# A frequency filter with a SwiGLU layer behind it: other filter tiles, a third stage-A buffer, moved x loads, and a last step in halves

## The chip, the cores and the metric

The kernel runs on one core of a Trainium2 chip, in a single launch. The metric is the device time of that core in microseconds (us). Engines are named as in the profile: PE is TensorE, with PEld for its weight loads, DVE is VectorE, ACT is ScalarE, POOL is GpSimd and SP is SyncE, which here only issues transfers. PSUM is the memory that PE writes its results to; SBUF is the memory that the engines share.

## What is computed

The input x has 8 sequences of 3008 rows by 256 columns. Each sequence is filtered in the frequency domain, then every row goes through an RMS norm and a SwiGLU layer of width 1536:

```python
X = np.fft.rfft(x, axis=1)                 # 8 x 1505 x 256
Y = X * (filt_r + 1j * filt_i)[None]       # filters: 1505 x 256
y = np.fft.irfft(Y, n=3008, axis=1).reshape(8 * 3008, 256)
xn = y / np.sqrt(np.mean(y * y, axis=-1, keepdims=True) + 1e-6) * rms_g
g = xn @ w_gate                            # 256 x 1536
out = (g / (1 + np.exp(-g)) * (xn @ w_val)) @ w_out
```

Inputs and output are float32; the kernel multiplies in float16 and accumulates in float32.

## The kernel before, in words

**The transform.** 3008 = 47 x 64, and the Fourier transform is done as two smaller ones, each a matmul with a constant table. For sequence b these calls follow one another, and the names are used from here on:

- `x_load(b, c)` (L173), c = 0 to 3: a quarter of the sequence's rows comes in, converted to float16, by a transfer issued from POOL (L185). Four `xc` buffers.
- `a_unit(b, i)` (L200), i = 0 to 11: the 64-point transform of two groups of rows, one matmul to `psa` (L205) and a copy to tile `t1` by ACT or DVE (L194 and L196 are the two lines of the copy helper). Three units fill one `t1`; there are two `t1` buffers.
- `z_store(b, c)` (L208): that `t1` goes to a scratch area in HBM, `z_tmp`, issued from SP; `t2_load(b, c)` (L215) brings it back with the axes exchanged, into one of four `t2` buffers (L217, SP).
- `b_unit(b, i)` (L232), i = 0 to 15: the 47-point transform, four matmuls to `psb` (L237), times the filter on DVE in two parts (`s_part`, L227 and L230); `add_unit` (L264) adds them on POOL into `ss`. Four units of sequence 1 are `b_soft` (L243), with the filter on POOL.
- `yt_load(b, g)` (L269): `ss` of two units is turned by a transposing transfer from SP into `yt`.
- `bi_unit(b, i)` (L276): the 47-point inverse, four matmuls to `psi` (L281) and a copy to `uu`. `t4_load(b, c)` (L292) turns a quarter of `uu` into `t4`, again by a transposing transfer from SP.
- `n_unit(b, m, i)` (L302), m = 0 to 5: the 64-point inverse, one matmul to `psn` (L310) and a copy to `y` on ACT. `sq_unit` (L314) sums the squares on ACT, `stat_unit` (L321) makes the row factor `rho` on POOL, `xt_unit` (L331) applies it on POOL, and `tr_unit(b, m)` (L341) turns the result by a transposing transfer from SP into `xn`, the input of the layer.

**The layer.** Rows go in 48 groups (b, m) of 512 (384 in the last group of an even sequence), each with 12 blocks jt of 128 of the 1536 middle columns. Such an item (b, m, jt) is a *slot*; there are 576, and slot 72 is the first of sequence 1. `gv` (L504) makes two matmuls each to `pg` and `pv` (L517), silu on ACT (L521) and the product `hh` on DVE (L522). `down` (L525), two slots later, adds four matmuls (three in a group of 384) to `po` (L534); at jt = 11 ACT and DVE copy the two halves of `po` to tile `o` (L539, L540), and `o_store` (L543) sends it out from SP (L546, and L549 for one more row in odd sequences).

**The head.** Sequence 0 has no earlier slots to hide in, so it runs straight, with forms of its own: `a0_unit` and `tr0_unit` make `t2` on PE without the scratch area, `yt0_unit` turns on PE, and `fill(n)` (L430) issues n matmuls that nobody reads, in PE's empty places. The filters come in here too. `f_load(i)` (L372) brings the rows of the filters in on POOL's queue: i = 0 the first 1024 rows of filt_i as 128 partitions of eight rows, i = 1 those of filt_r, i = 2 the remaining rows of both on 60 partitions each and the last row of each by itself. `f_unit(i, rg, dh)` (L388) transposes four of the eight rows of a tile on PE to `psf` (L394) and copies them into the filter table `ff`, in an order of rows that the pairing of the two transforms asks for: two copies at rg = 1 and four at rg = 0, twice that at i = 2; dh = 0 on ACT, dh = 1 on DVE. `f_neg` (L414) negates a part of `ff` on POOL. Then a loop over p (L630 to L637) runs b_unit, yt0_unit, bi_unit and fill of sequence 0 interleaved.

**The order.** From slot 0 on a planner places the calls of later sequences into slots: `a_plan`, `b_plan` and `norm_plan` ask `at` for a slot, and `fit` moves a call to a later slot while the PSUM bank is taken or ACT or DVE have too much in that stretch. The wanted slots are lists written out by hand (`at_`, `b_at`, `lags`, `n_at`); `lags` are the slots from a b_unit to its bi_unit. `t4_load` and `n_unit` of sequences 1 and 2 count from the last bi_unit. An engine and a queue take their instructions in the order in which the program issues them: a call that waits on SP or POOL holds up the calls behind it. Each of the two queues keeps eight semaphores for its transfers, and the n-th waits until the (n-8)-th has landed. From sequence 4 on, the plan repeats every 72 slots.

Of the kernel before, what the change touches and what calls it, by code (L numbers as in the profile page):

```python
# [10 lines left out]
FP32 = mybir.dt.float32  # L11
# [5 lines left out]
N = 3008  # L17
N1 = 47
# [4 lines left out]
B = 8  # L23
# [76 lines left out]
def kernel(  # L100
# [23 lines left out]
    glob = ctx.enter_context(tc.tile_pool(name="glob", bufs=1))  # L124
    stg = ctx.enter_context(tc.tile_pool(name="stg", bufs=4))
    xp = ctx.enter_context(tc.tile_pool(name="xp", bufs=4))
    t1p = ctx.enter_context(tc.tile_pool(name="t1p", bufs=2))
    t2p = ctx.enter_context(tc.tile_pool(name="t2p", bufs=4))
    sp = ctx.enter_context(tc.tile_pool(name="sp", bufs=4))
    ytp = ctx.enter_context(tc.tile_pool(name="ytp", bufs=4))  # L130
    t4p = ctx.enter_context(tc.tile_pool(name="t4p", bufs=4))
# [34 lines left out]
    def raw(src, row, ap):  # L166
        return bass.AP(tensor=src.tensor, offset=src.offset + row * D, ap=ap)
# [20 lines left out]
    def bank(i, name):  # L188
        pool, tag = ((psM, "mx"), (psG, "pg"), (psV, "pv"), (psB, "mb"))[i]
        return pool.tile([P, 512], FP32, tag=tag, name=name)  # L190

    def copy(eng, out, in_, scale=None):
        if eng == "A":
            nc.scalar.activation(out=out, in_=in_, func=AXT.Copy, **({} if scale is None else {"scale": scale}))  # L194
        elif scale is None:
            nc.vector.tensor_copy(out=out, in_=in_)  # L196
        else:
            nc.vector.tensor_scalar(out=out, in0=in_, scalar1=scale, scalar2=None, op0=ALU.mult)
# [11 lines left out]
        nc.sync.dma_start(dst, st[b]["t1"][c])  # L210

    def t2_tile(b, c):
        st[b]["t2"][c] = t2p.tile([KR, KC, D], FP16, tag="t2", name="t2")

    def t2_load(b, c):  # L215
        t2_tile(b, c)
# [59 lines left out]
    def bi_unit(b, i, eng="A", bk=0):  # L276
        g, dh = divmod(i, 2)
        yt = st[b]["yt"][g]
        ps = bank(bk, "psi")[:, 0:4 * KR].rearrange("p (k j) -> p k j", k=4)
        for k in range(4):  # L280
            nc.tensor.matmul(ps[:, k, :], yt[0:KR, k, dh, :], wi[:, 4 * g + k, :], start=True, stop=True)  # L281
        dst = uu[:, :, dh, 16 * g:16 * g + 16].rearrange("p c (k m) -> p c k m", k=4)
        copy(eng, dst, ps.rearrange("p k (c m) -> p c k m", c=H))
        done[b] += 1
        if done[b] == K2 // 2:
            half = uu[:, H - 1, :, :].rearrange("p e (k m) -> p e k m", k=K2)
            if b % 2:
                nc.gpsimd.tensor_copy(out=half[:, :, :, 2:4], in_=left)
            else:
                nc.gpsimd.tensor_copy(out=left, in_=half[:, :, :, 0:2])  # L290
# [76 lines left out]
        copy(eng, st[0]["t2"][c][:, 4 * r:4 * r + 4, :].rearrange("p k (e d) -> p k e d", e=2), ps)  # L367

    fst = {}
    FT = (NF - 1) // KC - P  # L370

    def f_load(i):  # L372
        t = stg.tile([P, KC, D], FP32, tag="stg", name="fs")
        fst[i] = t
        for f, src in ((0, filt_i), (1, filt_r)):
            if i < 2:
                if f == i:
                    nc.gpsimd.dma_start(t.rearrange("p a d -> p (a d)"), raw(src, 0, [[KC * D, P], [1, KC * D]]))
            else:
                if f == 0:  # L380
                    nc.vector.memset(t[32:64], 0.0)
                nc.gpsimd.dma_start(t[64 * f:64 * f + FT].rearrange("p a d -> p (a d)"),
                                    raw(src, KC * P, [[KC * D, FT], [1, KC * D]]))
        if i == 2:
            for f, src in ((0, filt_i), (1, filt_r)):
                nc.gpsimd.dma_start(t[64 * f + FT:64 * f + FT + 1, 0, :], raw(src, NF - 1, [[D, 1], [1, D]]))

    def f_unit(i, rg, dh):  # L388
        t = fst[i]
        r0 = 4 * rg  # L390
        ps = bank(1 + dh, "psf").rearrange("p (a q) -> p a q", a=4)
        for a in range(4):
            n = P if i < 2 else 64 + FT + (r0 + a == 0)
            nc.tensor.transpose(ps[:, a, 0:n], t[0:n, r0 + a, ds(dh * P, P)], idf[0:n, 0:n])  # L394
        e = "AV"[dh]
        fk = ff[:, dh].rearrange("p (t k) c -> p t k c", k=8)
        for f in ((i,) if i < 2 else (0, 1)):
            o = SL * (1 + f)
            if i < 2:
                v = ps.rearrange("p a (q s) -> p s a q", s=8)  # L400
                lo, hi, nh = slice(o, o + 16), slice(o + H, o + H + 16), 16
            else:
                v = ps[:, :, 64 * f:64 * f + 64].rearrange("p a (q s) -> p s a q", s=8)
                lo, hi, nh = slice(o + 16, o + H), slice(o + H + 16, o + 2 * H - 1), 7
            copy(e, fk[:, :, r0:r0 + 4, lo], v[:, 0:4])
            if rg:
                copy(e, fk[:, ::-1, 1:5, hi][:, :, ::-1, :], v[:, 4:8, :, 0:nh])
            else:
                copy(e, fk[:, ::-1, 5:8, hi][:, :, ::-1, :], v[:, 4:8, 1:4, 0:nh])
                copy(e, fk[:, 1:4, 0, hi][:, ::-1, :], v[:, 5:8, 0, 0:nh])  # L410
                n0 = nh + (i == 2)
                copy(e, ff[:, dh, 0, hi.start:hi.start + n0], v[:, 4, 0, 0:n0])

    def f_neg(k0, n):  # L414
        for dh in range(2):
# [12 lines left out]
        copy(eng, st[0]["yt"][g][0:KR, :, dh, :], ps)  # L428

    def fill(n):  # L430
        ps = psO.tile([P, 512], FP32, tag="po1", name="pf")
        for _ in range(n):
            nc.tensor.matmul(ps, wa, ss3[0].rearrange("p k e q -> p (k e q)")[:, 0:512], start=True, stop=True)

# [62 lines left out]
                                    in1=y[:, h, :].rearrange("p (q e t) -> p q e t", q=2, e=2), op=ALU.mult)  # L497
        st[0]["xn"][m] = xn

    SPLIT = ((0, 0, 0),)  # L500
    hh_of = {}
    po_of = {}

# [39 lines left out]
    def o_store(b, m):  # L543
        o3 = po_of.pop((b, m))
        w = 3 if m == 5 else 4
        nc.sync.dma_start(raw(out, b * N + 4 * m, [[N1 * D, N2], [H * D, 2], [1, w * D]]),  # L546
                          o3[:, 0:w, :].rearrange("p q d -> p (q d)"))
        if m == 5 and b % 2:
            nc.sync.dma_start(raw(out, b * N + H - 1, [[N1 * D, N2], [-N * D, 2], [1, D]]), o3[:, 3, :])  # L549
# [25 lines left out]
    with tc.manual_schedule():  # L575
# [35 lines left out]
        for g in range(8):  # L611
            tr0_unit(g, E[g % 2])
        for i in range(3):
            for rg in range(2):
                for dh in range(2):
                    f_unit(i, rg, dh)
        f_neg(0, 8)
        wo_load(0)
        f_neg(8, 8)
# [8 lines left out]
        for p in range(UN + 4):  # L628
            if p < UN:
                b_unit(0, p, (0, 3)[p % 2])  # L630
                s_part(0, p, 1)
            if 2 <= p < UN + 2:
                yt0_unit(p - 2, "AV"[p - 2 == UN - 1], 1)
            if p >= 4:
                bi_unit(0, p - 4, "AV"[p in (UN + 1, UN + 3)], 2)
            if p >= UN + 1:
                fill(1)  # L637
        t4_first()
# [20 lines left out]
        def at(slot, fn, *a):  # L659
            todo = (late if fn == q_unit else plan).setdefault(slot, [])  # L660
            if fn in front:
                todo.insert(0, (fn, a))
            else:
                todo.append((fn, a))
# [29 lines left out]
        def a_plan(b, slots):  # L694
            for i in range(12):
                opts = []
                for k in "MB":
                    opts.append((k, "A", ((k, 0, 1), ("A", 0, 0.6))))
                    opts.append((k, "V", ((k, 0, 1), (k, 1, 1), ("V", 0, 0.68))))
                k, e, need = min(opts, key=lambda o: fit(slots[i], *o[2], keep=False))  # L700
                s = fit(slots[i], *need)
                at(s, a_unit, b, i, e, 0 if k == 'M' else 3)
                if i % 3 == 2:
                    at(s + 1, z_store, b, i // 3)
                    if b + 1 < B:
                        at(max(s + 2, 18 + 4 * (i // 3)), x_load, b + 1, i // 3)
            return s + 1

        def b_plan(b, slots, lags, soft=()):
# [30 lines left out]
        for b in range(1, B):  # L740
            t = (b - 1) * 72
            if b == 1:
                z = a_plan(b, [i for i in range(12)])
                b_at, lags = [z + 7 + 7 * i // 5 for i in range(16)], (8, 8)
                soft = range(2, 16, 4)
            elif b == 2:
                z = a_plan(b, [28 + 3 * i for i in range(12)])
                b_at, lags, soft = [z + 10 + 5 * i // 2 for i in range(16)], (8, 9), ()
            else:
                at_ = [t - 87 + 4 * i for i in range(12)]  # L750
                z = a_plan(b, [s - (s % JT == 1) for s in at_])
                b_at, lags, soft = [t - 26 + 4 * i for i in range(16)], (8, 12), ()
            assert z + 3 <= b_at[0] - 4
            end = b_plan(b, b_at, lags, soft)
            for c in range(4):
                at(end + 1 + (3 * c if b < 3 else c), t4_load, b, c)
            n_at = end + 8 if b < 3 else t + 51
            assert n_at >= end + 4
            for m in range(6):
                norm_plan(b, m, (n_at + 8 * m, n_at + 8 * m + (4 if b > 1 else 2)), (2, 3, 7) if b > 1 else (2, 3, 6))  # L760
# [46 lines left out]
```

## Time and profile before

| | us |
|---|---|
| three runs before | 888.25, 888.74, 893.54; median 888.74 |
| the profiled execution's own time | 889.17 |
| its span in the profile | 887.3 |
| PE busy in it | 857.8 |
| PE idle before 52.7 | 14.3 |
| PE idle from 172.4 to 879.2 | 2.2 |
| half-clock record | 168.63 to 172.05 |

The profile is of one execution. A row of the timeline has the start, the busy time, the engine, the line, the operation with its output and inputs, and how many instructions are put together; a bracket at its end says how long the engine was idle before them and what ended that. A row of the waits says engine and line, what ended the wait, the total, the count and the longest. Times count from the start of the span. Where slots are in time: slot 24 begins at 89.7 on ACT, 57 at 144.1, 60 at 150.9, 72 at 164.9.

### The profile page before, as it was taken

The numbers are of one execution on the slowest core, as the hardware profiler recorded it, in microseconds if no ns is written. First come the engines' busy times: TensorE is split into PE (matmuls) and PEld (weight loads), VectorE is DVE, ScalarE is ACT, GpSimd is POOL, SyncE is SP. The second block draws the span as 40 slices with busy tenths as digits, with TensorE's granted clock in tenths as the row PEclk, the third lists the DMA queues.
The fourth block names the chain that finished last, engine by engine and source line by source line (L and its number), as shares of the span: only waits on it lengthen the run. The fifth ranks groups of instructions, "written<-read, shape, count | busy, mean of one in ns | idle before, by whom it ended". The sixth has DMA issues, their size and how long they took to land.

```text
span 887.3 us, 17016 instructions
## 1 busy us (share of the span) xinstructions
PE 857.8 (97%) x6130; PEld 532.1 (60%) x6130; DVE 565.5 (64%) x948; ACT 612.7 (69%) x1332; POOL 296.4 (33%) x340
## 2 busy tenths in 40 slices
PE   5889898899999999999999999999999999999997
PEld 4755565556666666666666666666666666665554
DVE  4946665476666666667667676766766666555554
ACT  4767676678678866887568865787657765677443
POOL 3812761355124431444124341343204440132000
PEclk9999999999999999999999999999999999999999
DMA  9956768865756658565755656654384341521101
GB/s 244 272 110 148 150 117 188 180 137 118 156 121 121 138 104 149 135 115 131 146 108 126 131 108 140 128 129 90 98 161 90 65 90 46 116 57 48 60 24 48
DMA packets 198645, 107.52 MB, mean 121 GB/s; under 512 B 159306, under 2 KB 183496, under 8 KB 198184
## 3 DMA queue, kind: packets, MB, share of 16 engines
q1 hardware_dynamic: 190608, 86.24, 43.8%
q0 software_dynamic: 7952, 20.19, 12.2%
q8 instruction: 48, 0.79, 0.4%
q14 instruction: 37, 0.30, 0.1%
HBM read 45.32 MB, written 35.65 MB: 91 GB/s over the span
## 4 chain that ended last, share of the span: by engine, by line
PE 85%; DMA 6%; DVE 3%; ACT 2%; POOL 2%; issue 1%; SPq 0%; POOLq 0%; ACTq 0%; DVEq 0%
PE po L534 25%; PE pg L517 25%; PE pv L517 24%; PE psb L237 2%; PE psi L281 2%; PE psn L310 2%; PE psa L205 2%; DMA fs<-in_filt_r_dram 2%; DMA yt<-ss 2%; DVE hh L522 1%; ACT sg L521 1%; DMA z_tmp<-t 1%; DMA t<-z_tmp 1%; DVE o L540 1%; DMA xc<-in_x_dram 1%
## 5 line engine op out<-in xcount | busy, mean ns | idle before, releaser
L522 DVE TENSOR_TENSOR hh<-pv,sg 128x512 f16<-128x512 f32 (+2 forms) x577 | 391.6, 679 | 295.1 <-ACT sg L521 212.6
L521 ACT ACTIVATE sg<-pg 128x512 f16<-128x512 f32 (+2 forms) x577 | 337.4, 585 | 227.3 <-PE pg L517 223.0
L534 PE MATMUL po<-wo,hh 128*128 128x256 f16 x2256 | 343.8, 273 | 2.3 <-DVE o L540 1.1
L517 PE MATMUL pg<-xn,wg 128*128 128x512 f16 (+2 forms) x1154 | 338.6, 375 | 0.2 <-DVE xn L495 0.2
L517 PE MATMUL pv<-xn,wv 128*128 128x512 f16 (+2 forms) x1154 | 338.2, 375 | 0.0
L534 PEld LDWEIGHTS <-hh 128*128 128x128 f16 x2256 | 212.3, 98 | 116.6 <-issue 7.0
L517 PEld LDWEIGHTS <-wv 128*128 128x128 f16 x1154 | 113.1, 98 | 131.2 <-issue 1.1
L264 POOL TENSOR_TENSOR ss<-s,s 128x384 f16<-128x384 f16 x112 | 101.8, 910 | 263.7 <-DVE s L230 237.9
L517 PEld LDWEIGHTS <-wg 128*128 128x128 f16 x1154 | 112.7, 98 | 15.2 <-issue 1.1
L336 POOL TENSOR_TENSOR xt<-y,rho 128x1024 f16<-128x1024 f32 (+1 forms) x46 | 85.3, 1854 | 3.0
L318 ACT ACTIVATE junk<-y 128x256 f16<-128x256 f32 x180 | 74.2, 412 | 2.8
L227 DVE TENSOR_TENSOR s<-psb,ff 128x384 f16<-128x384 f32 x124 | 67.8, 547 | 2.2 <-PE psb L237 2.2
L230 DVE TENSOR_TENSOR s<-psb,ff 128x384 f16<-128x384 f32 x124 | 67.8, 547 | 0.0
L194 ACT ACTIVATE uu<-psi 128x384 f16<-128x384 f32 x126 | 61.3, 486 | 2.7 <-PE psi L281 1.7
L194 ACT ACTIVATE y<-psn 128x512 f32<-128x512 f32 x96 | 56.2, 589 | 4.4
L281 PEld LDWEIGHTS <-yt 96*128 96x128 f16 x512 | 35.2, 97 | 29.8 <-DMA yt<-ss 3.4
L326 POOL TENSOR_SCALAR u<-ss 128x4 f32<-128x4 f32 (+1 forms) x46 | 8.9, 193 | 130.4 <-ACT junk L318 130.2
L328 POOL TENSOR_TENSOR rho<-u,mhalf 128x4 f32<-128x4 f32 (+1 forms) x46 | 46.4, 1009 | 3.8
L237 PE MATMUL psb<-wb,t 96*128 96x96 f16 x496 | 41.5, 206 | 5.0 <-DMA t<-z_tmp 2.7
L281 PE MATMUL psi<-wi,yt 96*128 96x96 f16 x512 | 42.9, 205 | 2.3 <-DMA yt<-ss 1.8
L194 ACT ACTIVATE t<-psa 128x512 f16<-128x512 f32 x65 | 38.5, 596 | 7.9 <-PE psa L205 3.9
L237 PEld LDWEIGHTS <-t 96*128 96x128 f16 x496 | 29.1, 97 | 16.9 <-DVE s L230 5.6
(81 smaller groups left out, 364.4 us busy)
## 6 DMA issues: line engine op xcount, KB each, us to landing
out_dram<-o SPq DMA_DIRECT2D x40, 512.0 KB, 3.3
xc<-in_x_dram POOLq DMA_DIRECT2D x31, 384.0 KB, 6.3
z_tmp<-t SPq DMA_DIRECT2D x28, 384.0 KB, 2.7
t<-z_tmp SPq DMA_DIRECT2D x28, 384.0 KB, 6.0
out_dram<-o SPq DMA_DIRECT2D x8, 384.0 KB, 2.7
ws<-in_moe_w_gate_dram POOLq DMA_DIRECT2D x3, 512.0 KB, 8.9
ws<-in_moe_w_val_dram POOLq DMA_DIRECT2D x3, 512.0 KB, 9.5
fs<-in_filt_i_dram POOLq DMA_DIRECT2D x1, 1024.0 KB, 13.0
```

Source lines behind the costliest of these rows:

```text
L194: nc.scalar.activation(out=out, in_=in_, func=AXT.Copy, **({} if scale is None else {"scale": scale}))
L227: eng.tensor_tensor(out=o, in0=ps, in1=f1, op=ALU.mult)
L230: eng.tensor_tensor(out=o, in0=ps[:, :, ::-1, :], in1=f2, op=ALU.mult)
L237: nc.tensor.matmul(ps[:, ts(k, KR)], st[b]["t2"][kk // KC][:, kk % KC, ds(dh * P, P)], wb[:, kk, :], start=True, stop=True)
L264: nc.gpsimd.tensor_tensor(out=ss3[g % 3][:, :, dh, 0:KR], in0=s[0], in1=s[1], op=ALU.add)
L281: nc.tensor.matmul(ps[:, k, :], yt[0:KR, k, dh, :], wi[:, 4 * g + k, :], start=True, stop=True)
L318: nc.scalar.activation(out=junk, in_=y[:, i, ts(u, D)], func=AXT.Square, accum_out=ss[:, 2 * i + u:2 * i + u + 1])
L336: nc.gpsimd.tensor_tensor(out=xt[:, 0:n, :], in0=y.rearrange("p a (u d) -> p (a u) d", u=2)[:, 0:n, :], in1=rho[:, 0:n].unsqueeze(2).to_br ...
L517: nc.tensor.matmul(ps[:, 0:w], wt[:, dt_, ts(jt, P)], xn[:, q0:q1, dt_, :], start=(dt_ == 0), stop=(dt_ == 1))
L521: nc.scalar.activation(out=sg[:, c], in_=pg[:, 0:w], func=AXT.Silu)
L522: nc.vector.tensor_tensor(out=hh[:, c], in0=pv[:, 0:w], in1=sg[:, c], op=ALU.mult)
L534: nc.tensor.matmul(po[s4 // 2][:, s4 % 2, :], hh[:, ts(s4, P)], wo[:, jt, :], start=(jt == 0 and s4 % 2 == 0), stop=(jt == JT - 1 and (s4 ...
```

## The change

1. Pools: three `t1` buffers for two, three `t2` buffers for four; the fourth `t2` of sequence 0 sits in an `o` buffer.
2. Filters: three tiles of four-row groups that hold both filters, 128, 128 and 120 partitions. There are eight transfers on POOL's queue, before six, and the memset is gone. `f_unit(i, f, dh)` has four transposes as before and always four copies: 48 transposes and 48 copies in both kernels.
3. `fill` writes to the bank of `psn` instead of one of `po`. In the loop over p, the bi_unit at p = 17 is copied by ACT, before by DVE.
4. Placement: x_load(2, c) from slots 18, 22, 26, 30 to 19 to 22; x_load(3, c) from 47, 51, 54, 63 to 66, 72, 78, 84; x_load(4, c) from 67, 79, 98, 108 to 82, 93, 102, 111; a_unit(3, i) from slots between 57 and 106 to 73 to 109, with z_store(3, c) from 66, 78, 97, 107 to 81, 92, 101, 110.
5. `lags` of sequence 1 from (8, 8) to (9, 9). With that bi_unit(1, i) runs in slots 30 to 53 (before 29 to 50), t4_load(1, c) in 54, 57, 60, 63 (before 51, 54, 57, 60), n_unit(1, 0, i) in 61 and 63 (before 58 and 60) and tr_unit(1, 0) in 69 (before 66).
6. The last item of all, (7, 5, 11), is done in halves like the first, and the last `o_store` is three transfers: rows 0 and 1 and row 2 from SP, row 3 from ACT.

From sequence 4 on the plan is the same in both.

```diff
--- before.py
+++ after.py
@@ -124,8 +124,8 @@
     glob = ctx.enter_context(tc.tile_pool(name="glob", bufs=1))
     stg = ctx.enter_context(tc.tile_pool(name="stg", bufs=4))
     xp = ctx.enter_context(tc.tile_pool(name="xp", bufs=4))
-    t1p = ctx.enter_context(tc.tile_pool(name="t1p", bufs=2))
-    t2p = ctx.enter_context(tc.tile_pool(name="t2p", bufs=4))
+    t1p = ctx.enter_context(tc.tile_pool(name="t1p", bufs=3))
+    t2p = ctx.enter_context(tc.tile_pool(name="t2p", bufs=3))
     sp = ctx.enter_context(tc.tile_pool(name="sp", bufs=4))
     ytp = ctx.enter_context(tc.tile_pool(name="ytp", bufs=4))
     t4p = ctx.enter_context(tc.tile_pool(name="t4p", bufs=4))
@@ -210,7 +210,10 @@
         nc.sync.dma_start(dst, st[b]["t1"][c])
 
     def t2_tile(b, c):
-        st[b]["t2"][c] = t2p.tile([KR, KC, D], FP16, tag="t2", name="t2")
+        if b == 0 and c == 3:
+            st[b]["t2"][c] = op.tile([KR, KC, D], FP16, tag="o3", name="t2o")
+        else:
+            st[b]["t2"][c] = t2p.tile([KR, KC, D], FP16, tag="t2", name="t2")
 
     def t2_load(b, c):
         t2_tile(b, c)
@@ -367,49 +370,35 @@
         copy(eng, st[0]["t2"][c][:, 4 * r:4 * r + 4, :].rearrange("p k (e d) -> p k e d", e=2), ps)
 
     fst = {}
-    FT = (NF - 1) // KC - P
+    FR4 = 4
+    FT = (NF - 1) // FR4 - 2 * P
 
     def f_load(i):
-        t = stg.tile([P, KC, D], FP32, tag="stg", name="fs")
+        t = stg.tile([P, 2, FR4, D], FP32, tag="stg", name="fs")
         fst[i] = t
+        n = P if i < 2 else FT
         for f, src in ((0, filt_i), (1, filt_r)):
-            if i < 2:
-                if f == i:
-                    nc.gpsimd.dma_start(t.rearrange("p a d -> p (a d)"), raw(src, 0, [[KC * D, P], [1, KC * D]]))
-            else:
-                if f == 0:
-                    nc.vector.memset(t[32:64], 0.0)
-                nc.gpsimd.dma_start(t[64 * f:64 * f + FT].rearrange("p a d -> p (a d)"),
-                                    raw(src, KC * P, [[KC * D, FT], [1, KC * D]]))
-        if i == 2:
-            for f, src in ((0, filt_i), (1, filt_r)):
-                nc.gpsimd.dma_start(t[64 * f + FT:64 * f + FT + 1, 0, :], raw(src, NF - 1, [[D, 1], [1, D]]))
-
-    def f_unit(i, rg, dh):
+            if i == 2:
+                nc.gpsimd.dma_start(t[n:n + 1, f, 0, :], raw(src, NF - 1, [[D, 1], [1, D]]))
+            nc.gpsimd.dma_start(t[0:n, f].rearrange("p a d -> p (a d)"),
+                                raw(src, FR4 * P * i, [[FR4 * D, n], [1, FR4 * D]]))
+
+    def f_unit(i, f, dh):
         t = fst[i]
-        r0 = 4 * rg
-        ps = bank(1 + dh, "psf").rearrange("p (a q) -> p a q", a=4)
-        for a in range(4):
-            n = P if i < 2 else 64 + FT + (r0 + a == 0)
-            nc.tensor.transpose(ps[:, a, 0:n], t[0:n, r0 + a, ds(dh * P, P)], idf[0:n, 0:n])
+        ps = bank(1 + dh, "psf").rearrange("p (a q) -> p a q", a=FR4)
+        for a in range(FR4):
+            n = P if i < 2 else FT + (a == 0)
+            nc.tensor.transpose(ps[:, a, 0:n], t[0:n, f, a, ds(dh * P, P)], idf[0:n, 0:n])
+        v = ps.rearrange("p a (q s) -> p s a q", s=16)
+        fk = ff[:, dh].rearrange("p (t k) c -> p t k c", k=4)
         e = "AV"[dh]
-        fk = ff[:, dh].rearrange("p (t k) c -> p t k c", k=8)
-        for f in ((i,) if i < 2 else (0, 1)):
-            o = SL * (1 + f)
-            if i < 2:
-                v = ps.rearrange("p a (q s) -> p s a q", s=8)
-                lo, hi, nh = slice(o, o + 16), slice(o + H, o + H + 16), 16
-            else:
-                v = ps[:, :, 64 * f:64 * f + 64].rearrange("p a (q s) -> p s a q", s=8)
-                lo, hi, nh = slice(o + 16, o + H), slice(o + H + 16, o + 2 * H - 1), 7
-            copy(e, fk[:, :, r0:r0 + 4, lo], v[:, 0:4])
-            if rg:
-                copy(e, fk[:, ::-1, 1:5, hi][:, :, ::-1, :], v[:, 4:8, :, 0:nh])
-            else:
-                copy(e, fk[:, ::-1, 5:8, hi][:, :, ::-1, :], v[:, 4:8, 1:4, 0:nh])
-                copy(e, fk[:, 1:4, 0, hi][:, ::-1, :], v[:, 5:8, 0, 0:nh])
-                n0 = nh + (i == 2)
-                copy(e, ff[:, dh, 0, hi.start:hi.start + n0], v[:, 4, 0, 0:n0])
+        lo = SL * (1 + f) + 8 * i
+        hi = lo + H
+        n = 8 if i < 2 else 7
+        copy(e, fk[:, :, :, lo:lo + 8], v[:, 0:8])
+        copy(e, fk[:, ::-1, 1:4, hi:hi + n][:, :, ::-1, :], v[:, 8:16, 1:4, 0:n])
+        copy(e, fk[:, 1:8, 0, hi:hi + n][:, ::-1, :], v[:, 9:16, 0, 0:n])
+        copy(e, ff[:, dh, 0, hi:hi + 8], v[:, 8, 0, 0:8])
 
     def f_neg(k0, n):
         for dh in range(2):
@@ -428,7 +417,7 @@
         copy(eng, st[0]["yt"][g][0:KR, :, dh, :], ps)
 
     def fill(n):
-        ps = psO.tile([P, 512], FP32, tag="po1", name="pf")
+        ps = bank(0, "pf")
         for _ in range(n):
             nc.tensor.matmul(ps, wa, ss3[0].rearrange("p k e q -> p (k e q)")[:, 0:512], start=True, stop=True)
 
@@ -497,7 +486,7 @@
                                     in1=y[:, h, :].rearrange("p (q e t) -> p q e t", q=2, e=2), op=ALU.mult)
         st[0]["xn"][m] = xn
 
-    SPLIT = ((0, 0, 0),)
+    SPLIT = ((0, 0, 0), (B - 1, 5, JT - 1))
     hh_of = {}
     po_of = {}
 
@@ -543,6 +532,12 @@
     def o_store(b, m):
         o3 = po_of.pop((b, m))
         w = 3 if m == 5 else 4
+        if b == B - 1 and m == 5:
+            row = lambda q, n: raw(out, b * N + 4 * m + q, [[N1 * D, N2], [H * D, 2], [1, n * D]])
+            nc.sync.dma_start(row(0, 2), o3[:, 0:2, :].rearrange("p q d -> p (q d)"))
+            nc.sync.dma_start(row(2, 1), o3[:, 2, :])
+            nc.scalar.dma_start(raw(out, b * N + H - 1, [[N1 * D, N2], [-N * D, 2], [1, D]]), o3[:, 3, :])
+            return
         nc.sync.dma_start(raw(out, b * N + 4 * m, [[N1 * D, N2], [H * D, 2], [1, w * D]]),
                           o3[:, 0:w, :].rearrange("p q d -> p (q d)"))
         if m == 5 and b % 2:
@@ -611,9 +606,9 @@
         for g in range(8):
             tr0_unit(g, E[g % 2])
         for i in range(3):
-            for rg in range(2):
+            for f in range(2):
                 for dh in range(2):
-                    f_unit(i, rg, dh)
+                    f_unit(i, f, dh)
         f_neg(0, 8)
         wo_load(0)
         f_neg(8, 8)
@@ -632,7 +627,7 @@
             if 2 <= p < UN + 2:
                 yt0_unit(p - 2, "AV"[p - 2 == UN - 1], 1)
             if p >= 4:
-                bi_unit(0, p - 4, "AV"[p in (UN + 1, UN + 3)], 2)
+                bi_unit(0, p - 4, "AV"[p == UN + 3], 2)
             if p >= UN + 1:
                 fill(1)
         t4_first()
@@ -703,7 +698,7 @@
                 if i % 3 == 2:
                     at(s + 1, z_store, b, i // 3)
                     if b + 1 < B:
-                        at(max(s + 2, 18 + 4 * (i // 3)), x_load, b + 1, i // 3)
+                        at(max(s + 2, {1: 19 + i // 3, 2: 62 + 2 * i}.get(b, 0)), x_load, b + 1, i // 3)
             return s + 1
 
         def b_plan(b, slots, lags, soft=()):
@@ -741,13 +736,13 @@
             t = (b - 1) * 72
             if b == 1:
                 z = a_plan(b, [i for i in range(12)])
-                b_at, lags = [z + 7 + 7 * i // 5 for i in range(16)], (8, 8)
+                b_at, lags = [z + 7 + 7 * i // 5 for i in range(16)], (9, 9)
                 soft = range(2, 16, 4)
             elif b == 2:
                 z = a_plan(b, [28 + 3 * i for i in range(12)])
                 b_at, lags, soft = [z + 10 + 5 * i // 2 for i in range(16)], (8, 9), ()
             else:
-                at_ = [t - 87 + 4 * i for i in range(12)]
+                at_ = [72 + 3 * i if b == 3 else t - 87 + 4 * i for i in range(12)]
                 z = a_plan(b, [s - (s % JT == 1) for s in at_])
                 b_at, lags, soft = [t - 26 + 4 * i for i in range(16)], (8, 12), ()
             assert z + 3 <= b_at[0] - 4
```

## The prediction

> **What bounds the kernel now.** I read the header and the chain first, then PE in stretches of time, then the waits by total, last the timeline around each place where PE stands.
>
> ```profile
> span 887.3 us, 17016 instructions
> PE 857.8 (97%) x6130; PEld 532.1 (60%) x6130; DVE 565.5 (64%) x948; ACT 612.7 (69%) x1332; POOL 296.4 (33%) x340
> ...
> PE 85%; DMA 6%; DVE 3%; ACT 2%; POOL 2%; issue 1%; SPq 0%; POOLq 0%; ACTq 0%; DVEq 0%
> ```
> TensorE is the bound, so a change counts only where PE stands still or its clock is low. Stretches (start:end, length, then busy us of PE, PEld, DVE, ACT, POOL, granted clock, DMA share, GB/s) say where:
>
> ```profile
> 136.00:148.00 12.00, 10.09 (x62) 5.85 (x60) 4.84 (x7) 6.62 (x13) 0.59 (x1) 1.00 1.10 212
> ...
> 165.22:168.63 3.41, 0.76 (x9) 0.53 (x9) 0.91 (x2) 0.36 (x2) 1.20 (x1) 1.00 1.18 248
> 168.63:172.05 3.42, 3.42 (x13) 1.53 (x11) 1.64 (x4) 1.72 (x3) 0.06 (x1) 0.50 1.12 196
> 172.40:879.20 706.80, 704.59 (x4868) 433.00 (x4867) 459.52 (x745) 496.22 (x1074) 220.90 (x239) 1.00 0.51 108
> ```
> From 172.4 on, PE idles 2.2 us in 707: nothing to win there, and the order there is the same in both kernels. All that can move lies before 172.4 and behind 879.2. The waits (total, times, longest) and the places:
>
> ```profile
> ACT t L194 <- DMA z_tmp<-t: 2.6, 1, 2.6
> ...
> PE psb L237 <- DMA t<-z_tmp: 2.7, 1, 2.7
> ...
> PE psn L310 <- ACT t L194: 1.9, 1, 1.9
> ...
> PE psi L281 <- DMA yt<-ss: 1.8, 2, 1.1
> ```
> ```profile
> 22.35 3.38 DVE L196 COPY ff<-psf 128x256 f32<-128x256 f32 x12 [0.19 <-PE psf L394]
> 45.22 0.33 PE L281 MATMUL psi<-wi,yt 96*128 96x96 f16 x4 [0.36 <-ACT uu L194]
> 47.28 0.59 PE L433 MATMUL pf<-ss,wa 128*128 128x512 f16 x2 [0.52 <-DVE t4f L196]
> ...
> 156.89 0.65 POOL L185 DMA_DIRECT2D xc<-in_x_dram  x1
> 156.97 1.28 SPq L345 DMA_TRANSPOSE xn<-xt  x1
> ...
> 167.96 0.34 PE L237 MATMUL psb<-wb,t 96*128 96x96 f16 x4 [2.65 <-DMA t<-z_tmp]
> ...
> 881.28 0.33 PEld L534 LDWEIGHTS <-hh 128*128 128x128 f16 x4 [0.39 <-DVE hh L522]
> 881.94 0.69 DVE L540 COPY o<-po 128x512 f32<-128x512 f32 x1 [0.71 <-PE po L534]
> ...
> 883.28 0.60 SPq L549 DMA_DIRECT2D out_dram<-o  x1
> ```
> Three kinds of stall carry the middle: inverse units waiting for a transpose, one n_unit waiting for stage A's buffer, and one b_unit waiting 2.65 us at slot 72, after which the clock record stands at 0.50 for 3.41 us.
>
> **The change, part by part.** The sum is made against the profiled execution's own 889.17 us (span 887.3); the median, 888.74, is 0.43 below it.
>
> *1. Filter stage.* The 48 transposes stay; PE issues them from 21.27, about 0.114 us each, so not before 26.75. Copies: before 6, 6 and 12 for each engine and tile (DVE 12 in 3.38 us), after 8, 8, 8. A unit now has 256, 192, some 56 and 8 columns; by rows of those widths .37+.295+.155+.10 = .92 us, six units per engine from 22.35 give 27.87, against 28.52 for the last copy now: −0.6. Bounds 0 (the eight DMAs on POOL's queue, before six, land as late as now: last at 25.22 with PE waiting 0.64 us for filt_r) and −0.9. f_neg follows on POOL and wi, the w and wo loads issue behind it, with eight lanes in that queue; the first inverse unit at 31.9 and the first gain at 35.8 have 3 us and more of cover, and beyond that each us late costs one.
>
> *2. Fill bank and bi(13).* The unit at p=17 goes from DVE to ACT: bank 0 is then freed by ACT's copy 44.26–44.75, yt(15) on DVE ends at 44.83, so psi at 45.22 can go at about 44.9: −0.35 (0 to −0.36, the shown wait). The fill of 47.28 leaves DVE's t4f bank: −0.43 (0 to −0.52).
>
> *3. Inverse units of sequence 1.* Lags 8,8 become 9,9: one slot more, about 1.5 us, against waits of 0.68 (103.70) and 1.12 (109.63), and x(2) moves out of 97–110: −1.76 (0 to −1.8). x(2) now lies together in slots 19–22, at 81.5–86. There xn(0,2), needed at 89.0, landed at 87.64; I put it at 88–88.7, so 0; bounds 0 and +1.5 (landing half as late again as the 3.1 us row below). Each x issue costs POOL 0.59 to 0.65 us: four of them, 2.4 us, now stand between the first adds of sequence 1 (0.91 each) in six us of slots, so an add, and with it yt(1,0), is late by 2.4 us at most; with lag 9 its inverse unit has some 13 us. Cover gone, PE stands at slot 30 for what is over.
>
> *4. Third t1 buffer.* n_unit's matmul at 147.93 waited 1.92 behind ACT, ACT 2.58 for a z_store's landing. With three buffers the tile written at 147.28 was stored two stores earlier: −1.9. Bounds: 0 if that store is as late too, and no more than −1.92. t2p from 4 to 3 costs 0: sequence 0's fourth tile sits in an o buffer, and a later t2 tile waits for the reading of the third before it, which PE has done by then; cover gone, its load is late by the row of 8.13 us below.
>
> *5. Slot 72.* t2(2,0) was issued at 159.78 and landed at 167.91, 8.13 us; other t2 loads took 4.8 and 4.9 (76.43, 232.76). It ran with xn, z_store and x(3,3), x(4,0). Those x calls go to slots 84 and 82, a(3) leaves 57–106 for 73–109, so z(3) is gone from here. At 4.9 us it lands at 164.7, before 165.3: −2.65. The half clock then goes too: 3.41 us at 0.50 lose −1.7. Bounds for both: 0 and −4.36.
>
> *6. The new wait.* All n_units of sequence 1 sit three slots later: n_unit(1,0) at 63 instead of 60, tr_unit(1,0) at 69 instead of 66, but the gate matmul of item (1,0,0) still needs xn at slot 72. From psn to xn's issue was 6.2 us (150.75 to 156.97: copy, squares, then POOL .19, 1.04 and 1.89), 0.37 of it behind ACT's o copy at 154.10, which slot 63 comes after: 5.8. From that psn to slot 72 are eight slots of .98 (pg, pv and po at 0.33 each in a group of 384) and .55 of its own: 8.39. So PE stands L − 2.59, L being xn's time to landing:
>
> ```profile
> L345 SPq DMA_TRANSPOSE xn<-xt x1: 1277/1277/1277, 157.0 to 157.0; - x1
> ...
> DMA to landing us min/median/max: 6.9/6.9/6.9
> ```
> The same view at 195.6 has 3.1. What differs is an x load issued 0.08 us ahead; three other cases of x issued 0.4–0.6 us ahead read 7.17–7.48, the largest anywhere 9.55 (99.04). In the changed order x_load(3,0) and (3,1) stand on POOL right behind xt_unit(1,0), so they issue with this transpose again. I take 6.9, the nearest row: stall 4.3 (0.5 at 3.1; 4.9 at 7.5; 7.0 at 9.55). Queued behind the waiting gate matmul are its value matmul, silu, hh and down, thus all of PE. On SP the next behind xn are a z_store and t2 loads with slots of cover; POOL's next is rho of m=1, 8 slots from need.
>
> A stall of 2.65 was followed by 3.41 us at half clock, one of 1.92 (147.93) was not: +1.7 after a stall of 4.3 (0 to +3.4, none or two such stretches).
>
> The Trainium skill, "TensorE: Matmul & The Clock Gate", on oscillation, gates the clock only after an idle window of about 3.4 us. The row above has half clock after 2.65 us, so the measurement decides; by the rule alone item 5 would not be owed the 1.7 and item 6 would be, which makes the sum 1.7 later.
>
> *7. x(3), x(4), a(3) and z(3) elsewhere.* PE's work is the same, in slots where PE does not wait. The eight x issues move on POOL past the rho and xt of (1,0), (1,1) and (1,2), which start that much earlier; the adds of sequence 2 behind them (one a 2.5 slots) get 0.6 us each in front, hidden by the lags of 8 and 9 slots. On SP z(3) moves behind t2(2) and the first three xn of sequence 1, a z_store issue of 0.32 to 1.33 us in front of the next xn, which has a slot of its own and 12 slots until it is read. I take 0 (−0.5 to +1, as for a copy that meets a full bank, 0.37 at 154.10, twice).
>
> *8. The end.* With the last item in halves, hh's last half ends about 0.27 earlier (880.96 for 881.23), down about 881.02 for 881.29. First store waits for ACT's o alone: issue 882.05–882.1, not 882.69; the last leaves at 882.7 not 883.28, as DVE's half feeds two queues at once: −0.58, landing +2.46 as now. Bounds 0 (the store on ACT's queue slower than SP's 0.60) and −0.9.
>
> Sum: −0.6 −0.35 −0.43 −1.76 −1.9 −4.36 + 4.3 + 1.7 −0.58 = −4.0. 889.17 − 4.0 = 885.2; on the median's scale 884.8.
>
> **The rivals.** A: no new wait. x(3,0) waits for its buffer or the transpose meets no x: L = 3.1, stall 0.5, no half clock; against the sum −3.8−1.7 = −5.5, so 879.2. For it: 3.1 is the reading without x. Against: x is directly behind xt on POOL.
> B, the other side: the same wait, with L at the 9.55 row and two half-clock stretches. Stall 7.0, clock 3.4: the sum is +0.4, so 889.1; it decides from L about 9.2. For it: two x loads, t2 and xn meet there at DMA share 1.18. Against: seven of eight rows are under 7.5.
> C: the waits of items 3 and 4 stay, as x loads were not their cause: −4.0+3.7, so 888.4. Against: both have a slot or a buffer more.
> The forecast without its half clock is 883.1.
>
> **How the numbers follow.** Chances: forecast 0.73 (0.2 of it without half clock), A 0.12, B 0.10, C 0.05. Predicted 884.8, the likeliest. The range 879.0–889.5 reaches from A to the middle of B and holds the ends of items 1–4 and 8 one by one; it leaves out the upper half of B and a sliver of A, with item 7's and item 3's ends on top of each other. Forecast's own: 882.5–887. About 1%, which a measurement of this kernel can tell, is 879.85 and 897.63: faster is most of A, 0.09; slower needs B with further lateness, 0.03; the same 0.88.
>
> **What would show it.** Right: a PE row at slot 72 (about 160) waiting for DMA xn 3–5 us, with the clock at 0.50 just behind; no waits on yt near 100, on ACT t near 145, on t2 in slot 72; last filter copy 0.5 us earlier; last store issued 0.6 us earlier relative to the last down. Wrong: xn landing in 3–4 us (A), over 9 (B), waits on yt or t still there (C), or a PE wait over 1 us at slots 19–24 or 73–111, which I priced at nothing.

## The result, and the profile after

| | before | after |
|---|---|---|
| median of 22 runs each, us | 890.32 | 894.98 |
| ratio, 95% interval | | 1.0054 (1.0038 to 1.0069) |
| the profiled execution's own time, us | 889.17 | 894.35 |
| its span, us | 887.3 | 892.6 |

The changed kernel is 0.5% slower, and the profile is 5.3 us longer. The head of the page and the engines of its chain, kernel after:

```profile
span 892.6 us, 17021 instructions
PE 858.7 (96%) x6134; PEld 533.2 (60%) x6134; DVE 563.3 (63%) x946; ACT 614.8 (69%) x1335; POOL 297.9 (33%) x342
...
PE 87%; DMA 5%; DVE 2%; POOL 2%; ACT 2%; issue 1%; POOLq 0%; ACTq 0%; DVEq 0%
```
PE has the same work, 858.7 us for 857.8. So again the time is where PE stands. Its waits for transfers between slot 0 and the end are one line now; the yt, the t2 and the stage-A lines are gone:

```profile
PE pg L506 <- DMA xn<-xt: 13.4, 2, 6.7
```
And the two places in the timeline, with POOL and SP ahead of the first, the filter copies and the end:

```profile
22.20 5.14 DVE L196 COPY ff<-psf 128x256 f32<-128x256 f32 x24 [0.19 <-PE psf L391]
...
79.54 1.90 POOL L185 DMA_DIRECT2D xc<-in_x_dram  x3
...
79.62 1.27 SPq L348 DMA_TRANSPOSE xn<-xt  x1
...
93.87 1.01 PE L506 MATMUL pg<-xn,wg 128*128 128x512 f16 x2 [6.66 <-DMA xn<-xt]
...
172.24 1.04 PE L506 MATMUL pg<-xn,wg 128*128 128x512 f16 x2 [6.74 <-DMA xn<-xt]
...
887.93 0.54 SPq L537 DMA_DIRECT2D out_dram<-o  x1
888.25 0.67 ACTq L539 DMA_DIRECT2D out_dram<-o  x1
888.58 0.54 SPq L538 DMA_DIRECT2D out_dram<-o  x1
```
The wait at 172.24 is the one that I forecast at slot 72, 6.74 us for 4.3. The wait at 93.87 is at slot 24, where I had priced the packed x loads at nothing: xn(0,2) was issued at 79.62, inside 1.2 us with three x loads, and landed 14.2 us later. That transpose in the view of the tile xn, first of the kernel before, then of the kernel after:

```profile
L345 SPq DMA_TRANSPOSE xn<-xt x1: 1273/1273/1273, 81.6 to 81.6; - x1
...
DMA to landing us min/median/max: 6.0/6.0/6.0
```
```profile
L348 SPq DMA_TRANSPOSE xn<-xt x1: 1275/1275/1275, 79.6 to 79.6; - x1
...
DMA to landing us min/median/max: 14.2/14.2/14.2
```
The same stretches by engine (columns as in the prediction), kernel after:

```profile
87.20:93.87 6.67, 0.01 (x2) 0.00 (x1) 0.51 (x2) 0.64 (x3) 5.64 (x6) 0.70 1.13 177
93.87:97.40 3.53, 3.53 (x16) 1.83 (x16) 1.56 (x3) 0.66 (x2) 0.65 (x2) 0.60 0.70 127
...
165.50:172.24 6.74, 0.01 (x1) 0.00 (x1) 0.56 (x1) 0.49 (x2) 0.00 (x0) 0.71 1.14 203
172.24:175.70 3.46, 3.46 (x15) 1.71 (x16) 1.16 (x2) 1.52 (x6) 0.68 (x2) 0.57 0.55 94
...
180.00:884.50 704.50, 702.61 (x4850) 431.61 (x4848) 458.65 (x744) 496.38 (x1075) 222.19 (x241) 1.00 0.53 110
```
PE does nothing for 6.7 us, twice, while the DMA share is 1.13 and 1.14, and the clock record is at 0.50 for 2.8 and 3.0 us of the work behind. From 180 on PE stands still for 1.9 us in 704.5, as little as before.

Where the 5.25 us come from, by the start of silu in numbered slots of both profiles: up to slot 1 −1.97; slots 1 to 30 +7.92 (the wait of 6.66, the rest the clock); 30 to 48 −1.40; 48 to 57 −0.29; 57 to 144 +1.62; 144 to 570 −0.06; to the end −0.57.

### The profile page after: what moved, and what is told of

Its sections match the earlier page's. It is cut to its first block, busy times and chain, and to the rows that moved or that the text cites. A ratio compares the mean times of both kernels' runs of the same rounds, so it can differ in the third digit from the quotient of the medians.

```text
span 892.6 us, 17021 instructions
## 1 busy us (share of the span) xinstructions
PE 858.7 (96%) x6134; PEld 533.2 (60%) x6134; DVE 563.3 (63%) x946; ACT 614.8 (69%) x1335; POOL 297.9 (33%) x342
## 4 chain that ended last, share of the span: by engine, by line
PE 87%; DMA 5%; DVE 2%; POOL 2%; ACT 2%; issue 1%; POOLq 0%; ACTq 0%; DVEq 0%
PE po L523 26%; PE pg L506 26%; PE pv L506 25%; DMA xn<-xt 3%; DMA xc<-in_x_dram 2%; PE psb L240 2%; PE psa L205 2%; PE psi L284 2%; PE psn L313 2%; DVE hh L511 1%; ACT sg L510 1%; DVE o L529 1%; POOL xt L339 0%; POOL ff L405 0%; PE psf L391 0%
```

## The experiments

Theory 1: x loads that are in flight with a transposing transfer make it land late, each by several us, and both new waits are that. Theory 2: the transposes are late for another reason, the new order on SP or the later tr_unit with its t2 loads. The first four kernels put x loads back, or move them alone.

**x2_spread**: the changed kernel, x_load(2, c) back.

```diff
-at(max(s + 2, {1: 19 + i // 3, 2: 62 + 2 * i}.get(b, 0)), x_load, b + 1, i // 3)
+at(max(s + 2, {1: 18 + 4 * (i // 3), 2: 62 + 2 * i}.get(b, 0)), x_load, b + 1, i // 3)
```


> The changed kernel with x_load(2, c) back in slots 18, 22, 26, 30. Theory 1 (x loads issued together with a transposing transfer delay it, about 4 us for each): only one x load stands beside xn(0,2) again, which lands in about 6 us instead of 14.2; the wait of 6.66 us at slot 24 falls under 1 us and the half clock behind it goes, so some 7 to 8 us less than the changed kernel, about 887. Theory 2 (xn is late for another reason, the new order of SP's queue or the t2 loads ahead of it): the wait at slot 24 stays at 6 us or more, time about 895. Slot 72 keeps its 6.7 us in both.

Measured: 887.15 us, ratio to before 0.9967 (0.9945 to 0.9989). xn(0,2) lands in 6.5 us, there is no wait at slot 24 and no half clock there; slot 72 keeps 6.59. Theory 1 at slot 24.

**x3_early**: the changed kernel, x_load(3, c) back.

```diff
-at(max(s + 2, {1: 19 + i // 3, 2: 62 + 2 * i}.get(b, 0)), x_load, b + 1, i // 3)
+at(max(s + 2, {1: 19 + i // 3}.get(b, 0)), x_load, b + 1, i // 3)
```


> The changed kernel with x_load(3, c) back in slots 47, 50, 54, 63, so that no x load is issued with xn(1,0). Theory 1: xn(1,0) lands in 3 to 5.5 us (t2 loads stand beside it still), the wait of 6.74 us at slot 72 falls to 0.5 to 3 us, 5 to 8 us less with the clock, 887 to 890. Theory 2 (the later tr_unit and the t2 loads are enough): the wait stays over 4 us and the clock record goes to 0.5 again. With three t1 buffers no wait of n_unit near 148 in either; if one is back, the x loads were its cause.

Measured: 889.34 us, ratio 0.9998 (0.9969 to 1.0027). xn(1,0) lands in 4.9 us, the wait at slot 72 is 1.88, with no half clock; slot 24 keeps 6.66. A n_unit near 155 waits 1.59 us for its t4, which now meets x(3,2). Theory 1 again.

**both**: both edits.

```diff
-at(max(s + 2, {1: 19 + i // 3, 2: 62 + 2 * i}.get(b, 0)), x_load, b + 1, i // 3)
+at(max(s + 2, 18 + 4 * (i // 3)), x_load, b + 1, i // 3)
```

> Both edits together, everything else as in the changed kernel. Theory 1: both waits gone or small; the sum of the parts that my prediction counted as gains stays, about 9 us under the kernel before: 879 to 883, ratio 0.990 to 0.994. Theory 2: about 895, or 887 if only one of the places obeys.

Measured: 882.22 us, ratio 0.9916 (0.9884 to 0.9947). Of PE's waits for xn there is left, kernel both:

```profile
PE pg L506 <- DMA xn<-xt: 1.3, 1, 1.3
```
Two placements of x loads turn 0.5% slower into 0.8% faster.

**b_x2burst**: the kernel before, with the packed x loads alone.

```diff
-at(max(s + 2, 18 + 4 * (i // 3)), x_load, b + 1, i // 3)
+at(max(s + 2, 19 + i // 3 if b == 1 else 0), x_load, b + 1, i // 3)
```


> The kernel before with one edit: x_load(2, c) in slots 19, 20, 21, 22. Theory 1: xn(0,2) lands in 12 us or more, a new wait of 5 to 7 us at slot 24 and a stretch at half clock behind it, less the two yt waits (1.8 us): 5 to 7 us slower, about 895. Theory 2: no new wait at slot 24, time 887 to 889.

Measured: 895.43 us, ratio 1.0077 (1.0052 to 1.0102). One edit to the old kernel makes the wait, kernel b_x2burst:

```profile
96.12 1.01 PE L517 MATMUL pg<-xn,wg 128*128 128x512 f16 x2 [6.12 <-DMA xn<-xt]
```
xn(0,2) lands in 13.7 us. The yt waits near 100 are gone as well, with lags (8, 8). The x loads are out of the way there, but PE's stall just ahead may have helped; no run parts the two. Theory 2 has fallen for slot 24.

**x2_two**: the version both, with two x loads beside xn(0,2) for one.

```diff
-at(max(s + 2, 18 + 4 * (i // 3)), x_load, b + 1, i // 3)
+at(max(s + 2, (19, 20, 26, 30)[i // 3] if b == 1 else 0), x_load, b + 1, i // 3)
```


> The version with both sets of x loads put back, and x_load(2, 1) alone moved from slot 22 to slot 20, so that two x loads are issued with xn(0,2), not one and not three. Theory 1, each x load costs about 4 us: xn(0,2) lands between the 6.0 us beside one and the 14.2 us beside three, at 9.5 to 10.5; the wait at slot 24 was the landing less 7.5 us, so 2 to 3 us. Rival: the delay comes only when x loads fill all they can (four of them), then xn lands in 6 to 7 us and there is no wait.

Measured (one execution, 883.45 us): the transpose, in the view of the tile xn, kernel x2_two:

```profile
L348 SPq DMA_TRANSPOSE xn<-xt x1: 1273/1273/1273, 80.0 to 80.0; - x1
...
DMA to landing us min/median/max: 9.8/9.8/9.8
```
PE waits 2.23 us at slot 24. With the kernels above: 6.0 beside one x load (both), 9.8 beside two, 14.2 beside three (the changed kernel), 3.8 and 4.4 us for the second and the third. The two ends repeat: beside one x load issued with it xn(0,2) took 5.98 to 6.52 us in eight profiles, beside three 13.17 to 14.73 in six.

**x2_after**: the version both, with the x loads behind the add of slot 21 on POOL.

```diff
-at(max(s + 2, 18 + 4 * (i // 3)), x_load, b + 1, i // 3)
+at(max(s + 2, 22 + i // 3 if b == 1 else 0), x_load, b + 1, i // 3)
```


> The same version with x_load(2, c) in slots 22, 23, 24, 25: again four x loads in one burst, but behind the add of slot 21 on POOL, so issued 4 us after xn(0,2). Theory 1 (what counts is what is in flight beside the transpose): xn(0,2) lands in 3 to 4 us, no wait at slot 24; yt(1,0) and t2 take the burst instead and land in 7 us or more, which lag 9 covers, or PE waits up to 2 us at slot 30. Rival (the burst itself does it, wherever it is): a wait of 3 us or more at slot 24.

Measured (one execution, 886.68 us), the same view, kernel x2_after:

```profile
L348 SPq DMA_TRANSPOSE xn<-xt x1: 1275/1275/1275, 80.6 to 80.6; - x1
...
DMA to landing us min/median/max: 3.7/3.7/3.7
```
No wait at slot 24. Only two of the four loads came as a pair (85.1), the others at 93.2 and 95.7, so it isn't the burst that I meant; but with no x load beside it the transpose takes 3.7, so the first costs 2.3. The 4 us more than both (7.2 between the two profiles) are mostly at another place: t4 beside x(3,2) landed in 14.5 us, where both had 7.7 for the same three transfers, and a n_unit waited 4.70, with half clock behind. What makes that difference was not found.

**b_lags**: the kernel before, with the other `lags` alone.

```diff
-b_at, lags = [z + 7 + 7 * i // 5 for i in range(16)], (8, 8)
+b_at, lags = [z + 7 + 7 * i // 5 for i in range(16)], (9, 9)
```

> The kernel before with one edit: lags (9, 9) for sequence 1, which puts tr_unit(1,0) into slot 69 and leaves x_load(4,0) behind xt_unit(1,0) on POOL. Theory 1: the two yt waits (1.8 us) go, and xn(1,0) lands beside one x load in 6 to 7 us: a new wait of 3 to 4 us at slot 72, the t2 wait there partly under it; 887 to 891. Rival: the later slot alone costs nothing, no wait for xn at slot 72.

Measured (one execution, 888.37 us): xn(1,0) beside one x load takes 7.2 us, the wait at slot 72 is 3.78, of the yt waits 0.39 is left, and the half clock behind slot 72 is there again. At slot 72, with t2 loads as well, the landing was 4.3 with no x load (both), 7.2 with one, 9.8 with two (the changed kernel). The later transpose makes the wait possible, and the x loads make its size.

**no_moves**: the changed kernel with every call placed as before.

```diff
-at(max(s + 2, {1: 19 + i // 3, 2: 62 + 2 * i}.get(b, 0)), x_load, b + 1, i // 3)
+at(max(s + 2, 18 + 4 * (i // 3)), x_load, b + 1, i // 3)
-b_at, lags = [z + 7 + 7 * i // 5 for i in range(16)], (9, 9)
+b_at, lags = [z + 7 + 7 * i // 5 for i in range(16)], (8, 8)
-at_ = [72 + 3 * i if b == 3 else t - 87 + 4 * i for i in range(12)]
+at_ = [t - 87 + 4 * i for i in range(12)]
```


> The changed kernel with the whole placement as before (x loads, lags, stage A of sequence 3); what is left of the change are the pools, the filter tiles, the bank of fill, the copy of the inverse unit at p = 17 and the halves at the end. My prediction's items 1, 2, 4 and 8 alone: 0.6 + 0.35 + 0.43 + 1.9 + 0.58 = 3.9 us under the kernel before, or 4.4 with the 1.97 us that the head showed. The wait of n_unit near 148 is gone (third buffer), the yt waits (1.8) and the t2 wait at slot 72 with its half clock stay. Rival for item 4: the third buffer does nothing and it was the x loads' place that removed the wait; then the wait of 1.9 is there, and the gain is 2 to 2.5.

Measured: 884.38 us, ratio 0.9943 (0.9921 to 0.9965). Its waits, with no n_unit waiting for ACT's `t` among them, kernel no_moves:

```profile
PE psb L240 <- DMA t<-z_tmp: 2.4, 1, 2.4
...
PE psi L284 <- DMA yt<-ss: 1.9, 3, 1.5
```
So everything except the placement is worth 0.6%, and the placement as a whole, as it was made, costs 1.1% (1.0054 against 0.9943). The third buffer does remove the wait at 148, with the x loads where they were. In b_lags, with two buffers, that wait is gone as well: either is enough.

**lag8**: the version both, with the old lags.

```diff
-b_at, lags = [z + 7 + 7 * i // 5 for i in range(16)], (9, 9)
+b_at, lags = [z + 7 + 7 * i // 5 for i in range(16)], (8, 8)
```

> The version with both sets of x loads put back, with lags (8, 8) again for sequence 1, so tr_unit(1,0) in slot 66. If the lags matter: the wait for xn at slot 72 (1.29) goes, the yt waits near 100 and 107 (0.7 and 1.1) come back, 882.5 to 884. If only the x loads mattered, no yt wait is back and it is 881.

Measured: 880.32 us, ratio 0.9897 (0.9878 to 0.9915), the lowest of all. No wait for xn at slot 72, and the price, kernel lag8:

```profile
107.40 0.34 PE L284 MATMUL psi<-wi,yt 96*128 96x96 f16 x4 [2.02 <-DMA yt<-ss]
```
Its interval overlaps that of both, so which lags are better isn't told. The wait moves from one place to the other. From no_moves this kernel differs by the later slots of a(3) alone, with the z(3) and x(4) that follow it: the wait for t2 at slot 72 falls from 2.35 to 0.21, and the ratio from 0.9943 to 0.9897, with intervals that don't meet. So one part of the placement is a gain. A wait that only moves is also what came of **n_earlier**, the version both with the n_units of sequence 1 two slots earlier.

```diff
-n_at = end + 8 if b < 3 else t + 51
+n_at = end + (6 if b == 1 else 8) if b < 3 else t + 51
```


> The same version with the n_units of sequences 1 two slots earlier (6 slots behind the last inverse unit, before 8), so tr_unit(1,0) in slot 67. Theory 1: the wait of 1.29 us that is left at slot 72 goes, unless n_unit then waits for t4 (1.6 us in one run above): 880 to 882, 1 us under the version above. Rival: xn(1,0) is late with the t2 loads whatever its slot, and 1 us or more stays.

Measured: 882.38 us, 0.9906 (0.987 to 0.9941). The wait for xn goes from 1.29 to 0.75, and a n_unit waits 1.53 for t4, a b_unit 0.93 for t2: nothing gained.

**sp_store**: the version both, with the last of the three stores on SP's queue.

```diff
-nc.scalar.dma_start(raw(out, b * N + H - 1, [[N1 * D, N2], [-N * D, 2], [1, D]]), o3[:, 3, :])
+nc.sync.dma_start(raw(out, b * N + H - 1, [[N1 * D, N2], [-N * D, 2], [1, D]]), o3[:, 3, :])
```


> The version with both sets of x loads put back, with the last of the three stores at the end on SP's queue, not ACT's. The end is then bound by three issues on one queue of about 0.55 us each: from the end of the last down to the end of the span about 0.3 to 0.5 us more than the 5.08 there. Rival: landing takes its time from the last bytes, and it is the same.

Measured (one execution): 5.02 us from the end of the last down to the end, for 5.08 in both. The last issue is at 876.42, 1.67 us behind the end of the last down (1.09 in both), and the end comes no later, so the last issue doesn't set it; the rival holds.

**after_fill**, **fill_24** and **fill_72**: the changed kernel with 30 unread matmuls ahead of the two waits, or of one.

```diff
+def cover(bk):
+    ps = bank(bk, "pc")
+    for _ in range(30):
+        nc.tensor.matmul(ps, wa, wg[:, 0, 0:512], start=True, stop=True)
+at(23, cover, 3)
+at(71, cover, 0)
```


> The changed kernel with 30 matmuls that nobody reads (6.5 us of PE) in front of the last step before slot 24 and before slot 72, where PE stands idle 6.7 us in the changed kernel. If the half clock follows PE's idleness, both records at 0.50 go, and the time falls by the 1.4 and 1.5 us that the two stretches cost, less what the last of the added matmuls delays: 892 for 895. If it follows the transfers or anything else, the records stay and the time is the same or longer.

> The changed kernel with the 30 unread matmuls only before slot 24. If the half clock is a loss of its own, the record at slot 24 goes and with it 1.4 us: 893.5 for 895. If PE's work there makes xn(0,2) later or holds the downs of slots 21 and 22 past its landing, more than the clock gives is lost: 896 to 898, with slot 24 later by 1 to 3 us in the profile.

> The same before slot 72 only. A loss of its own: 893.5 for 895; matmuls that hold later work: 896 to 898, with slot 72 later in the profile.

Measured: 898.23 us (1.0054 to 1.012 of before) with both, 897.38 (1.0059 to 1.0098) and 893.54 (1.0015 to 1.0045) with one. In each profile the half clock is gone just where the matmuls are: it follows PE's idleness, not the transfers. In time that isn't shown to pay. fill_72 is 1.4 us under the changed kernel, with intervals that overlap. In fill_24 slots 24 to 30 take 9.59 us, for 10.48, but xn(1,0) at slot 72, beside the same transfers, took 12.1 us to land in its profile and PE waited 9.03. Whether fill_24's matmuls cause that by shifting what meets what, or whether 9.8 and 12.1 are both common, stays open; so does the time of after_fill, whose profiled execution (893.52) is well under its other runs.

## Why the prediction was wrong, by its own steps

I forecast −4.0 us in the profile and it is +5.2. The profiled execution settles it item by item.

- **Item 3, x(2) in slots 19 to 22, is the step that failed**: "I put it at 88–88.7, so 0; bounds 0 and +1.5". It cost a wait of 6.66 us and 1.3 us of half clock. Two things were wrong in it. I took slots for times ("at 81.5–86"). Nothing on POOL between xt_unit(0,2) and the first add waits for PE, so the first three loads left at 79.54, 80.19 and 80.72, the moment that xt_unit was done, beside xn(0,2), which xt_unit also sets free. And I carried the row for one x load (6.0) over to four. b_x2burst and x2_spread show both signs of it, x2_two the size of one load. In the same item I counted what four x issues cost POOL, 2.4 us; that was covered, as I had it, and what the transfers cost each other was the larger part.
- **Item 6**, the wait at slot 72, was right in place and cause, and short in size: the prediction names two x loads and prices the landing with the row at 156.97 (6.9), as one with a single x load 0.08 us ahead. A second stood 0.90 us behind it (rows below). In the changed kernel the two left back to back, 162.33 and 162.98, and the landing was 9.8, the stall 6.74 for 4.3 (the cover was 3.05, not 2.59). This is rival B's mechanism, and just past the 9.2 from which I let it decide. x3_early and both show that the x loads make it; with none the stall is 1.88 and 1.29.
- **The half clock**: 1.7 behind one stall was about right; 1.5 at slot 72, and 1.3 at slot 24, which I did not have.
- **Item 1**, the filter tiles: the sign right, the size half. DVE's last copy ends at 27.3, not at 27.87 as I had worked out (28.52 before): −1.2 for −0.6. The 24 copies in 5.14 us show .86 a unit for my .92, and the b_unit behind them starts 1.19 earlier (28.32 for 29.51).
- **Item 2** gave what the two waits held: both are gone, and of the head's −1.97 the remaining 0.78 is just the 0.35 + 0.43. That closeness is luck: slot 1 begins at 51.88 to 53.70 in the thirteen profiles with the new head, at 54.69 to 55.83 in the three with the old one. The gain is clear, its parts to 0.1 us are not.
- **Items 3 (yt), 4 and 5** came as forecast: the waits are gone in the changed kernel. Their causes were less single than I wrote. For the yt waits the lags alone were nearly enough (b_lags, 0.39 left), and the moved x loads alone perhaps too (b_x2burst, behind its stall); for item 4 the buffer was enough (no_moves), and so was a later n_unit (b_lags). For item 5 a(3) with its x and z transfers is what counts: in no_moves, with old places, the t2 wait stays (2.35), and in lag8, with these alone moved, it is 0.21.
- **Item 8** gave −0.57 for −0.58, but not by its reason: the ACT queue has no part in it (sp_store). With the halves the last down ended 0.23 earlier from slot 570 on, and the end came 0.34 sooner after it. The second part is not shown to be the halves': b_lags, with the old end, took 5.12 us from the last down to the end, and n_earlier, with the new one, 5.38 (before 5.42, after 5.08).

The sum by what was measured: the forecast's −4.0, +7.9 for slot 24, +2.2 for slot 72 with its clock, −0.6 for the head is +5.5, against +5.2.

The two x loads by item 6's row, on POOL, kernel before:

```profile
156.89 0.65 POOL L185 DMA_DIRECT2D xc<-in_x_dram  x1
157.87 0.59 POOL L185 DMA_DIRECT2D xc<-in_x_dram  x1 [0.33 <-PE psa L205]
```
The Trainium skill, "DMA: Bandwidth & Descriptors", under "Issuing engines are not separate DMA queues", says that transfers issued from several engines run on the same 16 DMA engines and interleave. The runs agree and add a price for this pair: at slot 24 each of up to three loads that POOL issued with the transpose, 0.53 to 0.65 us apart, made it land 2.3 to 4.4 us later. Being in flight is not all that counts: a second load 0.97 or 0.98 us behind the first, as in these rows, added little or nothing at the first transpose of sequence 1, which landed in 6.9, 6.1 and 6.5 us (before, no_moves, b_x2burst). What makes that difference was not tested.

On the clock, the same skill's "TensorE: Matmul & The Clock Gate", on oscillation, has idle gaps of more than about 3.4 us as the limit. Here 2.23 us were enough in x2_two and 2.35 were not in no_moves; the rows below decide.

## What to carry to other kernels

A call's place in the program is no time: a transfer on a queue that waits for nothing leaves at once, and it leaves together with whatever the same event set free, so look for what both stand behind. When a transfer is moved, list what will be in flight beside each transfer that has a reader with little slack, and count them; the cost of issuing was the small part here. And when waits go at several places at once, test the parts by themselves: here gains (0.6% without the placement) and losses (1.1% by it) sat in different parts of one change, and the x loads and lags of the old kernel with the rest of the change gave one 1.0% under it (lag8).

## What the runs showed of the hardware

**A clock that looks at fixed stretches.** The records at 0.50 are 3.41, 6.83 or 10.24 us long (the one at the end of a run is cut off), so one, two or three steps of a raster, a fixed grid in time. From slot 0 on, PE's busy time in the step just before tells whether the next one is at half clock. Such steps, first of x2_two, then of no_moves and of the kernel before:

```profile
87.29:90.70 3.41, 1.18 (x9) 0.53 (x7) 0.76 (x2) 1.18 (x4) 2.61 (x4) 1.00 0.83 164
90.70:94.11 3.41, 3.41 (x17) 1.87 (x16) 1.96 (x4) 0.90 (x2) 3.17 (x4) 0.50 0.36 99
```
```profile
160.06:163.47 3.41, 1.88 (x12) 0.88 (x9) 1.71 (x3) 1.49 (x4) 2.92 (x2) 1.00 1.09 278
163.47:166.88 3.41, 2.59 (x19) 1.58 (x20) 1.16 (x2) 1.78 (x4) 0.00 (x0) 1.00 1.23 221
```
```profile
144.75:148.16 3.41, 1.50 (x10) 0.71 (x9) 0.68 (x1) 0.88 (x2) 0.00 (x0) 1.00 1.25 170
148.16:151.57 3.41, 3.41 (x24) 2.20 (x23) 1.58 (x3) 3.34 (x10) 0.00 (x0) 1.00 0.92 188
```
Six steps at full clock with 0.54 to 1.33 us of PE had half clock behind them (before, after twice, x2_two, b_lags, x2_after); three with 1.50 to 1.92 had not (the two above and one in x3_early). The other profiles agree from slot 0 on: 0.00 to 1.23 us was followed by half clock, 1.50 and more was not. In the head it is less clean: steps with 1.58 (b_x2burst), 1.67 (b_lags), 1.68 (x2_after) and 1.73 us (no_moves), near 27, were followed by half clock, and 1.55 (b_lags) and 1.70 (x2_two) were not. So PE's busy time as the profile has it isn't the whole rule. In the layer, a wait of 2.35 us that falls into two steps (no_moves, 161.94 to 164.29) had no half clock behind it, and one of 2.23 inside one step (x2_two) was paid with 3.41 us at half clock. A stall's price depends on where it falls in the raster.

**Landing times vary beside the same transfers.** The same t4 transposes and x load took 7.7, 9.2 and 14.5 us to land in three kernels with equal orders there (both, n_earlier, x2_after), and 11.6 in sp_store, which is the kernel both up to its last store. xn(0,2) beside equal x loads, in contrast, repeated to within 1.6 us. A landing time from one profile is one draw.
